# Last projections in three PSUM banks, frequency tables in another buffer, and halves exchanged by DMA in all fifteen regular frequency groups

## The chip, the cores and the metric

One NeuronCore of one Trainium2 chip runs the whole program. The metric is device time in microseconds (us) of one execution, from launch to end; lower is better. The kernel before took 462.2 us (median of 3 runs, 462.19 to 463.9). Its profiled execution took 462.63 us.

## The reference

The input is one sequence `x` of 2048 positions with 640 features, all in float32. Two branches are computed from it and mixed by a gate of each position.

```python
x = A_x
g = _sigmoid((x * gate_w).sum(-1, keepdims=True))
a = _A_ref(x, A_wqkv, A_wo)
b = _B_ref(x, B_w_r, B_w_i)
return g * a + (1 - g) * b
```

Branch A is attention with 32 heads of 20 features. Each position looks at 8 positions: itself and those 2, 4, ... 14 before it. `qkv = x @ wqkv`, softmax over the 8 logits, weighted sum of the values, and a last product with `wo` (640 x 640).

Branch B is a filter in the frequency domain: `irfft2(rfft2(x) * (w_r + 1j * w_i))` over positions and features, with one complex weight for each of 2048 x 321 frequencies.

## The kernel before, in words

**Tiling.** Position `16 p + j` lies on partition `p` (128 of them) in tile `j` (16 of them). Even and odd `j` are two halves of the attention (`par` 0 and 1), since a position looks only at positions of its own parity.

**Projections** (`qkv`, line 707). `wqkv` is cut into 4 column blocks `hg`. For each parity and block there are 8 tiles (`jj`), one PSUM bank each, with 15 matmuls of 128x128 by 128x480: the input and the weights are each split into a high and a low float32r part, and three of the four products are summed over 5 chunks of the features. Block 0 has two columns more, for the gate. A finished tile is copied by ScalarE (`ev`), together with its gate column (`z<-qkv`), and two tiles go to DRAM (`qkvd`) in one DMA of ScalarE's queue. There are two `ev` buffers, so a copy may wait for the DMA of the copy two before. Unit `u = 4 * par + hg`; the last unit to be recorded is u = 4 (odd tiles, block 0), whose tiles are named `qkv4_0` to `qkv4_7`. All units take their PSUM banks from one ring of seven, `BP`.

**Attention** (`attend`, line 745). For each parity and 8 head pairs, VectorE multiplies keys and queries and reduces them to logits `L`, GpSimd multiplies values by the softmax (`pv`), VectorE reduces these to `o`, and SP stores `o` to DRAM (`od`). It fills VectorE and GpSimd for most of the run.

**Filter.** `cols` (line 849) transforms each `x` tile over the partitions into `zg`, whose 128 columns of a tile are 16 groups of 8. `freq(g)` (line 871) carries one group through the rest; groups run in the order 1, 2, 3, 0, 4, ... 15, staged four deep. It gathers the group (`zc`), transforms the features (`v` and `u`, three matmuls each, in banks 0 and 1), adds and subtracts them (`ab`), and transforms over the 16 tiles with a table `tb` (`x` in bank 2, `z` in banks 3 and 4). A complex weight needs the real and the imaginary half of each result, which stand on partitions 0 to 63 and 64 to 127, and also the same result with the halves exchanged and one negated. There are two ways to get it. A group in `EXCHANGED` (1 to 8 before) multiplies `x` and `z` by a sign on ScalarE into `X` and sends `X` with two DMAs of ScalarE's queue to the other half of `P`. Every other group multiplies again on TensorE with the exchanged table (`ix` and `iz`). Then GpSimd multiplies `P` by the weights `wp` (three rows of 321 in an exchanged group, two in another) and adds, VectorE makes `z` and the sum and difference `s`, TensorE transforms back (`g`, bank 5), and ScalarE writes the group back into `zg`. A group that isn't exchanged has one VectorE multiply more (`t`).

The tables of three groups come in one load `mm` (960 columns). Before, `mm` shares the two buffers `ev0` and `ev1` with the projections' copies.

**Ends.** Even projections by `wo` (`project_even`, line 1079) need only attention of even tiles and are spread among the groups. When all groups are done, `spatial` (line 997) transforms `zg` back (`oa`, `ob`, `ha`, `hb`), first for odd, then for even tiles. Last come the odd projections (`project_odd`, line 1095): five transposes `oTp`, thirty matmuls `woa` and `wob`, two VectorE operations and a store for each of 8 tiles.

**What sets the order.** The program is not issued as it is written. Every operation is recorded with the data that it touches (`Plan.record`, line 223; in the profile every one of them has line 639, so rows are told apart by the names of their tiles). `Plan.order` (line 277) then draws 60 random changes of priority from a generator seeded with `SEED`, lays out each by a model with a duration for each kind of operation, and keeps the one that ends earliest. Each engine then runs its list in that fixed order, so an instruction that waits holds all behind it on its engine.

Of the kernel before, what the change touches and what calls it, by code (L numbers as in the profile page):

```python
# [24 lines left out]
PERM = np.array([0, 320] + list(range(2, 320, 2)) + list(range(1, 320, 2)))  # L25

BP = (0, 1, 2, 3, 4, 5, 6)
BV, BU, BX, BZ, BG, BO = (0,), (1,), (2,), (3, 4), (5,), (6,)
PAGE = 512

# [437 lines left out]
                exec(*op.call)  # L468


TURNS, AGAIN, MOVE, SEED = 6, 60, 2.0, 0
DRAWS, SOONEST, LATER_BY = 3, 2.4, 0.6
ENGS = ("PE", "DVE", "ACT", "POOL", "SP")
RATE = 380e3
# [29 lines left out]
class Mixer:  # L504
# [17 lines left out]
    def places(self, pp, dr, sb):  # L522
        self.pp, self.sb = pp, sb
        qb = self.pp.tile([128, 512], F32, tag="qbank", name="qbank")
        self.qthird = [qb[:, GC * i : GC * i + GC] for i in range(3)]
        self.qturn = -1
        self.qkv_d = dr.tile([8, 6, ROWS, HC], F32, tag="dram_qkv", name="qkvd")
        self.o_d = [dr.tile([128, 8, D], F32, tag=f"dram_o{i}", name=f"od{i}") for i in range(2)]
        self.f_d = dr.tile([128, 8, 2, D], F32, tag="dram_f", name="fd")
        self.a_d = dr.tile([128, 8, D], F32, tag="dram_a", name="ad")  # L530
        self.ident, self.fc = (self.one(n, 128) for n in ("ident", "fc"))
        self.fct = self.one("fct", 2, 128)
        self.z, self.g, self.ng, self.nng = (self.one(n, NJ) for n in ("z", "g", "ng", "nng"))
        make_identity(self.nc, self.ident)
        self.low = self.one("low", 64)
        self.nc.gpsimd.memset(self.low, -1e9)

        def ring(*tags):
            return Ring(sb, *tags)

        def n(tag, k):
            return ring(*(f"{tag}{i}" for i in range(k)))


        self.kvr, self.Lr, self.qr, self.prr = n("kv", 6), n("L", 3), n("q", 2), n("pr", 2)
        self.mr, self.sr, self.orr, self.pvr = n("m", 2), n("s", 2), n("o", 2), n("pv", 2)

        self.xr, self.wr, self.evr, self.rawr, self.fr = n("x", 8), ring(*WPLACES), n("ev", 2), n("raw", 5), n("f", 2)
        self.er = ring("e0", "e1")

        self.zcr, self.vsr, self.mdr, self.mfr, self.wpr = n("raw", 2), ring("raw2"), n("ev", 2), ring("mf"), n("f", 2)
        self.abr, self.Pr, self.s12r, self.Xr = ring("x0", "x1"), ring("x2", "x3"), ring("x4", "x5"), ring("raw3", "raw4")
        self.p1r = ring("x6")

        self.wor, self.war, self.yar = ring("ya", "w7"), n("w", 7), ring("ya")
        self.otr, self.oTr = (ring("w7"), ring("w7", "kv2")), (ring("x7"), ring("x7", "pr0"))
        self.osr, self.hor, self.hyr, self.yer = n("raw", 3), n("x", 4), ring("x4", "x5"), ring("x6")
        self.yr, self.yir = ring("raw3", "raw4", "e0", "ya"), n("f", 2)
        self.banks = {}
# [75 lines left out]
    def warm(self):  # L635
# [3 lines left out]
        p.dve.memset(w, 0.0)  # L639
        b = self.ps(BP, "warmed")  # L640
        for _ in range(6):
# [15 lines left out]
    def load_w(self, st, hg):  # L657
# [4 lines left out]
        for t in range(5):  # L662
# [8 lines left out]
            if hg == 1 and (t > 2 or 1 in self.xT) or (hg, t, 1 in self.xT) in W_DVE:  # L671
                b = self.ps(BP, f"ws{t}")[:, 0:n]
                p.act.copy(b, raw)
# [8 lines left out]
    def load_x(self, st, pair, j):  # L682
# [15 lines left out]
        if st is None and j in XO_DVE:  # L698
            for c in (0, 320):
                b = self.ps(BP, f"xs{j}_{c}")[:, 0:320]  # L700
                p.act.copy(b, raw[:, c : c + 320])
# [5 lines left out]
    def qkv(self, par, hg):  # L707
        p, d = self.p, self.qkv_d
        n = 482 if hg == 0 else 480
        u = 4 * par + hg  # L710
        for jj in range(8):
            j = 2 * jj + par
            hi, lo = self.xT[j]
            b = self.ps(BP, f"qkv{u}_{jj}")
            terms = []
            for t in (0, 2, 1, 4, 3) if u + jj == 0 else range(5):
                x = slice(128 * t, 128 * t + 128)
                if u == 0 and (jj, t) in WHOLE:
                    terms.append((self.xraw[j][:, x], self.wraw[hg, t]))
                else:  # L720
                    terms += [(a[:, x], w[hg][t]) for a, w in ((hi, self.wh), (hi, self.wl), (lo, self.wh))]
            for i, (a, w) in enumerate(terms):
                p.pe.matmul(b[:, 0:n], a, w, start=(i == 0), stop=(i == len(terms) - 1))
            if jj % 2 == 0:
                ev = self.evr.next(f"ev{u}_{jj}", 6, 2, HC)
            p.act.copy(ev[:, :, jj % 2], b[:, 0:480].rearrange("p (i c) -> p i c", i=6))
            if hg == 0:
                p.act.copy(self.z[:, j : j + 1], b[:, 480:481])
            if jj % 2:
                to = bass.AP(  # L730
                    tensor=d.tensor,
                    offset=d.offset + (6 * u * ROWS + 7 + jj - 1) * HC,
                    ap=[[8 * HC, 128], [ROWS * HC, 6], [1, 2 * HC]],
                )
                p.act.dma_start(to, ev.rearrange("p i j c -> p i (j c)"))
# [113 lines left out]
    def cols(self, q):  # L849
        p = self.p  # L850
        f = self.folded[q]
        for t0, n in ((0, 2), (2, 2), (4, 1)):
            z = self.ps(BP, f"z{q}_{t0}")
            for i in range(2 * n):
# [16 lines left out]
    def freq(self, g):  # L871
# [53 lines left out]
        A.copy(P[:, 0], x)  # L925
        if g in EXCHANGED:
            X = self.Xr.next(f"X{g}", 2, 321)
# [8 lines left out]
        yield  # L936
        n = 3 if g in EXCHANGED else 2
        G.tensor_mul(P[:, 0:n], P[:, 0:n], wp[:, 0:n])
        G.tensor_add(P[:, 0], P[:, 0], P[:, 1])
        if g in EXCHANGED:  # L940
            V.tensor_mul(z, z, wp[:, 3])
# [201 lines left out]

ON_ACT = ("vt", "q")

EXCHANGED = tuple(range(1, 9))

POOL_PR = {u: (6,) for u in ((0, 3), (0, 4), (0, 5), (0, 7), (1, 0), (1, 1), (1, 3), (1, 4), (1, 5), (1, 7))}

# [52 lines left out]
```

## Time and profile before

| | before |
|---|---|
| median of 3 runs | 462.2 us |
| the profiled execution | 462.63 us |
| its span, first to last instruction | 460.9 us |
| TensorE weight loads (PEld), busy | 393.6 us |
| ScalarE, busy | 210.0 us |
| DMA moved | 108.53 MB, mean 235 GB/s |

The profile names the engines PE (TensorE, with PEld for its weight loads), DVE (VectorE), ACT (ScalarE), POOL (GpSimd) and SP. A row `iz<-ab,mm` is an instruction that writes tile `iz` from `ab` and `mm`. A float32 matmul appears as two records, so a count of x2 is one matmul. "idle before" is the time in which the engine stood still ahead of an instruction, with what released it. ACTq and SPq are DMA issues.

### The profile page before, as it was taken

How to read it: one execution, taken by the hardware profiler on the slowest of the kernel's cores; microseconds unless marked ns; L12 is line 12 of the kernel's file. 1: busy time of each engine (PE TensorE's matmuls, PEld its weight loads, DVE VectorE, ACT ScalarE, POOL GpSimd, SP SyncE). 2: the span in 40 equal slices, each digit the busy share in tenths (PEclk: the TensorE clock that was granted, in tenths of full speed). 3: DMA queues.
4: the chain of work that ended last, by engine and by line, in shares of the span. 5: the costliest groups of instructions: out<-in, count | busy, mean ns of one | idle time of the engine just before them, and what ended most of it. 6: DMA issues, size and time to landing. Idle time of an engine off the chain costs nothing.

```text
span 460.9 us, 7237 instructions
## 1 busy us (share of the span) xinstructions
PE 448.6 (97%) x2465; PEld 393.6 (85%) x2465; DVE 416.4 (90%) x547; ACT 210.0 (46%) x547; POOL 324.3 (70%) x264
## 2 busy tenths in 40 slices
PE   7899999999999999999999989999999999999997
PEld 4688888888889889899887779988888999998996
DVE  4599959999999999999999999999999996989584
ACT  5432435453326454257348656656445554332120
POOL 1001644999999969999799899788787888952200
PEclk9999999999999999999999999999999999999999
DMA  8999998869697988869979998886362321546733
GB/s 297 409 367 319 390 373 269 272 190 304 174 281 227 321 260 281 263 199 295 327 216 256 295 283 240 246 280 215 115 207 74 114 70 58 165 111 197 233 110 114
DMA packets 73124, 108.53 MB, mean 235 GB/s; under 512 B 21104, under 2 KB 50800, under 8 KB 73088
## 3 DMA queue, kind: packets, MB, share of 16 engines
q1 hardware_dynamic: 40768, 69.90, 47.6%
q10 hardware_dynamic: 31408, 34.18, 23.7%
q0 software_dynamic: 912, 4.00, 2.2%
q8 instruction: 19, 0.31, 0.3%
q14 instruction: 17, 0.14, 0.1%
HBM read 72.59 MB, written 32.84 MB: 229 GB/s over the span
## 4 chain that ended last, share of the span: by engine, by line
PE 88%; DMA 4%; DVE 3%; POOL 2%; ACT 1%; issue 1%; SPq 0%; ACTq 0%; POOLq 0%; DVEq 0%
PE qkv L639 43%; PE wob L639 8%; PE woa L639 8%; PE z L639 6%; PE g L639 4%; PE ob L639 3%; PE oa L639 3%; PE v L639 3%; PE u L639 3%; PE x L639 2%; PE oTp L639 2%; DMA raw<-in_wqkv 2%; PE ha L639 2%; PE hb L639 1%; DMA st<-in_xT 1%; POOL P L639 1%
## 5 line engine op out<-in xcount | busy, mean ns | idle before, releaser
L639 PE MATMUL qkv<-w,xo 128*128 128x480 f32 (+1 forms) x480 | 107.8, 383 | 0.0
L639 PE MATMUL qkv<-w,xe 128*128 128x480 f32 (+1 forms) x465 | 102.9, 382 | 1.7 <-ACT xe L639 1.0
L639 PEld LDWEIGHTS qkv<-w,xe 128*128 128x128 f32 x465 | 87.3, 188 | 17.5 <-ACT xe L639 2.4
L639 PEld LDWEIGHTS qkv<-w,xo 128*128 128x128 f32 x480 | 89.9, 189 | 13.9
L639 ACT COPY ev<-qkv 128x480 f32<-128x480 f32 x64 | 35.5, 557 | 49.9 <-PE qkv L639 38.1
L639 PE MATMUL woa<-wo,oT 128*128 128x320 f32 x240 | 52.0, 318 | 0.0
L639 PE MATMUL wob<-wo,oT 128*128 128x320 f32 x240 | 51.5, 316 | 0.0
L639 PEld LDWEIGHTS woa<-wo,oT 128*128 128x128 f32 x240 | 39.4, 188 | 0.3
L639 PEld LDWEIGHTS wob<-wo,oT 128*128 128x128 f32 x240 | 39.2, 188 | 0.4
L639 POOL TENSOR_TENSOR P<-P,wp 128x963 f32<-128x963 f32 (+1 forms) x16 | 30.5, 1904 | 8.5 <-ACT P L639 3.7
L639 POOL TENSOR_TENSOR w<-raw,w 128x480 fp32r<-128x480 f32 (+1 forms) x20 | 25.2, 1278 | 12.6 <-ACT w L639 12.5
L639 POOL DMA_DIRECT2D fd<-fx x6 | 4.3, 717 | 39.8 <-DVE fx L639 39.8
L639 POOL TENSOR_TENSOR yi<-yi,y 128x640 f32<-128x640 f32 x8 | 12.5, 1557 | 22.1 <-DMA yi<-ad 12.9
L639 ACT CAST oT<-oTp 128x384 fp32r<-128x384 f32 (+1 forms) x32 | 13.4, 428 | 31.2 <-PE oTp L639 18.3
L639 PEld LDWEIGHTS g<-mm,s 128*128 128x128 f32 x150 | 21.4, 190 | 3.7 <-ACT zg L639 0.5
L639 PE MATMUL v<-bt,zc 128*128 128x321 f32 (+2 forms) x96 | 22.2, 347 | 1.9 <-ACT vs L639 1.0
L639 PE MATMUL oa<-gt,zg 128*128 128x161 f32 (+1 forms) x96 | 23.0, 344 | 0.0
L639 PE MATMUL g<-mm,s 128*128 128x128 f32 x150 | 22.9, 275 | 0.1
L639 PE MATMUL ob<-gt,zg 128*128 128x161 f32 (+1 forms) x96 | 22.5, 344 | 0.0
L639 PE MATMUL u<-bt,zc 128*128 128x321 f32 (+2 forms) x96 | 21.6, 344 | 0.0
L639 PEld LDWEIGHTS v<-bt,zc 128*128 128x128 f32 x96 | 16.1, 189 | 6.0 <-ACT vs L639 1.2
L639 ACT CAST w<-raw 128x480 fp32r<-128x480 f32 (+1 forms) x30 | 17.3, 592 | 8.1 <-PE qkv L639 3.3
(306 smaller groups left out, 1101.9 us busy)
## 6 DMA issues: line engine op xcount, KB each, us to landing
qkvd<-ev ACTq DMA_DIRECT2D x32, 480.0 KB, 5.7
wp<-in_ws SPq DMA_DIRECT2D x16, 642.0 KB, 4.9
raw<-in_wqkv SPq DMA_DIRECT2D x25, 240.0 KB, 7.1
fx<-in_x SPq DMA_DIRECT2D x8, 641.0 KB, 8.9
ot<-od SPq DMA_DIRECT2D x16, 320.0 KB, 3.2
fd<-fx POOLq DMA_DIRECT2D x6, 640.0 KB, 7.7
f<-fd SPq DMA_DIRECT2D x6, 640.0 KB, 6.1
P<-X ACTq DMA_DIRECT2D x16, 160.5 KB, 4.2
```

The costliest lines, as they stand in the source:

```text
L639: p.dve.memset(w, 0.0)
```

## The change

The diff is whole but for headers.

```diff
 BP = (0, 1, 2, 3, 4, 5, 6)
+BL = (4, 5, 6)
 BV, BU, BX, BZ, BG, BO = (0,), (1,), (2,), (3, 4), (5,), (6,)
...
-TURNS, AGAIN, MOVE, SEED = 6, 60, 2.0, 0
+TURNS, AGAIN, MOVE, SEED = 6, 60, 2.0, 2
...
-        self.zcr, self.vsr, self.mdr, self.mfr, self.wpr = n("raw", 2), ring("raw2"), n("ev", 2), ring("mf"), n("f", 2)
+        self.zcr, self.vsr, self.mdr, self.mfr, self.wpr = n("raw", 2), ring("raw2"), ring("x6", "ev0"), ring("mf"), n("f", 2)
         self.abr, self.Pr, self.s12r, self.Xr = ring("x0", "x1"), ring("x2", "x3"), ring("x4", "x5"), ring("raw3", "raw4")
-        self.p1r = ring("x6")
...
-            b = self.ps(BP, f"qkv{u}_{jj}")
+            b = self.ps(BL if u == 4 else BP, f"qkv{u}_{jj}")
...
-EXCHANGED = tuple(range(1, 9))
+EXCHANGED = tuple(range(1, 16))
```

The eight tiles of the last projection unit rotate through banks 4, 5 and 6 instead of seven, so that banks 0 to 3 are no longer held by them. The first table `mm1` goes to `x6` and the next to `ev0`, in turn. Groups 9 to 15 exchange halves by DMA: `ix` and `iz` are built for group 0 alone. The new seed draws other priorities for the whole program, so the lists of all engines differ from their start on. The program has 1985 matmuls before and 1971 after.

Three places of the new order follow. First, TensorE at the end of the last projection unit. `qkv4_7` is its last tile; `v`, `u`, `x` and `z` with a number are steps of that frequency group. Before:

```order
L639 MATMUL qkv4_7_323<-w0_2_293,xo15_196 128x482 x3
L639 MATMUL v2_612<-bt_325,zc2_611 128x321
L639 MATMUL x1_607<-ab1_605,mm1_599 128x321
L639 MATMUL z1_608<-ab1_605,mm1_599 128x321
L639 MATMUL v2_612<-bt_325,zc2_611 128x161
L639 MATMUL v2_612<-bt_325,zc2_611 128x160
L639 MATMUL u2_614<-bt_325,zc2_611 128x321
L639 MATMUL u2_614<-bt_325,zc2_611 128x161
L639 MATMUL u2_614<-bt_325,zc2_611 128x160
L639 MATMUL qkv4_7_323<-w0_3_295,xo15_196 128x482 x3
L639 MATMUL qkv4_7_323<-w0_4_297,xo15_196 128x482 x3
L639 MATMUL v3_623<-bt_325,zc3_622 128x321
```

After:

```order
L639 MATMUL v3_623<-bt_325,zc3_622 128x321
L639 MATMUL x2_618<-ab2_615,mm1_599 128x321
L639 MATMUL v3_623<-bt_325,zc3_622 128x161
L639 MATMUL v3_623<-bt_325,zc3_622 128x160
L639 MATMUL z2_619<-ab2_615,mm1_599 128x321
L639 MATMUL qkv4_5_320<-w0_4_297,xo11_192 128x482
L639 MATMUL u3_625<-bt_325,zc3_622 128x321
L639 MATMUL u3_625<-bt_325,zc3_622 128x161
L639 MATMUL u3_625<-bt_325,zc3_622 128x160
L639 MATMUL qkv4_7_323<-w0_1_291,xo15_196 128x482 x3
L639 MATMUL qkv4_7_323<-w0_2_293,xo15_196 128x482 x3
L639 MATMUL qkv4_7_323<-w0_3_295,xo15_196 128x482 x2
```

Before, group 3 starts after the last projection; now groups 1, 2 and 3 have their `v` and `u` behind them while 12 matmuls of `qkv4_7` are still to come.

Second, TensorE at the last groups. `woa` and `wob` are matmuls of an even projection, `oTp` its transposes, `g` a group's transform back. Before:

```order
L639 MATMUL g13_0_813<-mm13_776,s13_802 128x128 x3
L639 MATMUL oTp0_859<-ident_69,ot8_857 128x128 x3
L639 MATMUL iz14_815<-ab14_797,mm13_776 128x321
L639 MATMUL g13_3_814<-mm13_776,s13_802 128x128 x2
L639 MATMUL x15_819<-ab15_812,mm13_776 128x321
L639 MATMUL z15_820<-ab15_812,mm13_776 128x321
L639 MATMUL oTp3_860<-ident_69,ot8_857 128x128 x2
L639 MATMUL ix15_821<-ab15_812,mm13_776 128x321
L639 MATMUL g14_0_822<-mm13_776,s14_817 128x128 x3
```

After:

```order
L639 MATMUL g12_3_791<-mm10_730,s12_779 128x128 x2
L639 MATMUL oTp0_852<-ident_69,ot10_850 128x128 x3
L639 MATMUL z15_808<-ab15_802,mm13_770 128x321
L639 MATMUL g13_0_803<-mm13_770,s13_792 128x128 x3
L639 MATMUL oTp3_853<-ident_69,ot10_850 128x128 x2
L639 MATMUL g13_3_804<-mm13_770,s13_792 128x128 x2
L639 MATMUL g14_0_810<-mm13_770,s14_805 128x128 x3
L639 MATMUL woa10_855<-wo0_327,oT10_851 128x320 x3
```

`ix` and `iz` are gone. After these rows stand the rest of `woa10`, two of `g14`, all 15 of `wob10` and three transposes ahead of the first matmul of `g15`; between `z14` and `g14` stand 30 projection matmuls, five of `g12`, five of `g13`, `x15`, `z15`, a third of `u15` and five transposes.

Third, VectorE ahead of the odd projections. `h`, `ha` and `y` are the even tiles' spatial step, `o4b6` the last of the attention, `oT` the transposed rows for an odd projection. Before:

```order
L639 SCALAR_TENSOR_TENSOR ha12_980<-ha12_980,ng_74,h12_982 128x161
L639 TENSOR_TENSOR y12_987<-ha12_980,h12_982 128x321
L639 TENSOR_TENSOR oT1_996<-oTp3_998,oT1_996 128x256
L639 TENSOR_TENSOR y12_987<-ha12_980,h12_982 128x319
L639 SCALAR_TENSOR_TENSOR h14_990<-ha14_988,ng_74,h14_990 128x161
L639 SCALAR_TENSOR_TENSOR h14_990<-ha14_988,nng_75,h14_990 128x160
L639 TENSOR_TENSOR oT1_996<-oTp0_997,oT1_996 128x384
L639 TENSOR_TENSOR oT3_1002<-oTp3_1004,oT3_1002 128x256
```

After:

```order
L639 TENSOR_REDUCE o4b6_597<-pv4b6_598 128x160
L639 TENSOR_TENSOR oT1_982<-oTp3_984,oT1_982 128x256
L639 SCALAR_TENSOR_TENSOR h12_968<-ha12_966,ng_74,h12_968 128x161
L639 SCALAR_TENSOR_TENSOR h12_968<-ha12_966,nng_75,h12_968 128x160
L639 SCALAR_TENSOR_TENSOR h14_976<-ha14_974,ng_74,h14_976 128x161
L639 SCALAR_TENSOR_TENSOR ha12_966<-ha12_966,ng_74,h12_968 128x160
L639 TENSOR_TENSOR oT1_982<-oTp0_983,oT1_982 128x384
L639 SCALAR_TENSOR_TENSOR h14_976<-ha14_974,nng_75,h14_976 128x160
L639 TENSOR_TENSOR oT3_988<-oTp3_990,oT3_988 128x256
```

The first `oT1` has moved ahead of all of `h12` and `h14`, and part of tile 12 (its last `ha12` and both `y12`) behind it.

## The prediction

> **What bounds the kernel now.** I read the page's busy shares first, then a table by stage, then the chain that ended last, then the waits of TensorE.
>
> ```profile
> PE 448.6 (97%) x2465; PEld 393.6 (85%) x2465; DVE 416.4 (90%) x547; ACT 210.0 (46%) x547; POOL 324.3 (70%) x264
> ```
>
> TensorE is busy for 448.6 of 460.9 us and VectorE for 416.4, so either can set the end. Which of them does depends on the stage. In the next view the columns are the stretch, its length, and the busy time of PE, PEld, DVE, ACT and POOL, then the granted clock (1.00, full speed, throughout), the share of the DMA engines and GB/s.
>
> ```profile
> 0.00:22.00 22.00, 17.49 (x64) 11.97 (x64) 9.81 (x16) 10.76 (x20) 1.99 (x9) 1.00 0.94 351
> 22.00:100.00 78.00, 78.00 (x357) 67.23 (x358) 71.25 (x85) 33.50 (x83) 39.19 (x34) 1.00 0.90 313
> 100.00:234.00 134.00, 134.00 (x693) 117.92 (x692) 132.62 (x117) 59.16 (x159) 124.76 (x99) 1.00 0.85 263
> 234.00:255.00 21.00, 19.22 (x98) 15.34 (x96) 20.83 (x27) 13.80 (x42) 19.89 (x18) 1.00 0.92 267
> 255.00:275.00 20.00, 18.50 (x101) 14.99 (x102) 18.65 (x32) 12.44 (x38) 17.41 (x14) 1.00 0.93 284
> 275.00:350.00 75.00, 74.93 (x463) 66.01 (x463) 72.68 (x115) 42.22 (x116) 61.58 (x52) 1.00 0.70 217
> 350.00:380.00 30.00, 30.00 (x191) 27.55 (x190) 29.90 (x30) 16.45 (x44) 26.41 (x21) 1.00 0.24 71
> 380.00:420.00 40.00, 38.99 (x247) 35.46 (x246) 33.06 (x66) 16.86 (x38) 28.36 (x22) 1.00 0.41 120
> 420.00:461.00 41.00, 37.51 (x263) 37.14 (x261) 27.63 (x68) 4.85 (x13) 4.70 (x3) 1.00 0.51 161
> ```
>
> From 22 to 234 us TensorE never stops. It stands 1.78 and 1.50 us in the two stretches in which the projections end and the groups begin, then runs without a break to 400. VectorE runs nearly as full until 380, then has slack. To see that a busy TensorE here is work and not waiting, I read pieces of the chain in the stage of the groups (start, length, what):
>
> ```profile
> 300.42 0.22 PE g L639 x2
> ...
> 303.81 0.54 PE iz L639 x2
> ...
> 305.12 0.22 PE oTp L639 x2
> ...
> 309.23 2.21 PE woa L639 x15
> ```
>
> The chain of that stage is TensorE throughout, matmul against matmul. So a matmul taken out of it is time off the span, as long as nothing else becomes late.
>
> **Matmuls removed.** Seven groups (9 to 15) lose `ix` and `iz`. The grouped rows of TensorE say how many that is, 14 records of each, two records a matmul:
>
> ```profile
> L639 PE MATMUL ix<-ab,mm 128*128 128x321 f32 x14 | 5.1, 444 | 0.0
> ...
> L639 PE MATMUL iz<-ab,mm 128*128 128x321 f32 x14 | 4.9, 434 | 0.0
> ```
>
> The 434 to 444 ns of a record overlap with the next record, so I price by the chain: 0.54 us a matmul. 14 x 0.54 = 7.6 us less, all of it from a stretch (275 to 350) in which TensorE is busy for 74.93 of 75 us.
>
> **Work put in their place.** The multiply of `P` on GpSimd grows from two rows of weights to three. ScalarE copies once less and signs twice, and VectorE loses `t`:
>
> ```profile
> L639 POOL TENSOR_TENSOR P<-P,wp 128x963 f32<-128x963 f32 x8 | 17.9, 2243 | 4.6 <-DMA P<-X 2.6 <-ACT L6a L639 1.5 <-ACT X L639 0.5
> ...
> L639 POOL TENSOR_TENSOR P<-P,wp 128x642 f32<-128x642 f32 x8 | 12.5, 1565 | 3.8 <-ACT P L639 3.7
> ...
> L639 ACT ACTIVATE X<-x,sign 128x321 f32<-128x321 f32 x8 | 4.3, 532 | 1.6 <-PE x L639 1.4
> ...
> L639 ACT COPY P<-ix 128x321 f32<-128x321 f32 x8 | 3.4, 427 | 3.8 <-PE ix L639 3.8
> ```
>
> The view of tile `t` gives minimum, median and maximum in ns, and the first and last start:
>
> ```profile
> L639 DVE TENSOR_TENSOR t<-z,wp x8: 481/484/490, 262.9 to 341.5; 128x321 f32<-128x321 f32 x8
> ```
>
> GpSimd gets 7 x (2.243 - 1.565) = 4.7 us more. In 275 to 350 it is busy for 61.58 of 75 us, which leaves 13.4 us; I cost it at nothing, and at up to 4.7 us if the attention's `pv`, queued behind it, has no slack. ScalarE gets 7 x (2 x 0.532 - 0.427) = 4.5 us and 14 DMA issues, beside 42.22 of 75 us busy: nothing. VectorE gets 7 x 0.484 = 3.4 us back.
>
> One rule of the Trainium skill speaks against the longer GpSimd multiply. SBUF — State Buffer, section "Who interferes with whom", says that a VectorE instruction with two SBUF inputs is shut out for the whole of a GpSimd instruction that reads SBUF. Read as if it held for every VectorE instruction, it would charge the 4.7 us to VectorE as well, and its 3.4 us gain would become a loss of 1.3; where VectorE sets the end, the time by it would be 462.2 + 1.3 = 463.5 us. By its own condition it spares the multiplies of the groups, whose other input is in PSUM, and the row of `t` agrees: 481 to 490 ns eight times over, beside a GpSimd that is busy 82% of that stretch.
>
> **The longer way of a half.** An exchanged half returns later than a matmul did, and TensorE's list is fixed, so the distance in its list between `z` and `g` must cover the way. The last exchanged group before, group 8, shows the whole way:
>
> ```profile
> 291.64 0.70 PE L639 MATMUL z<-ab,mm 128*128 128x321 f32 x2
> ...
> 292.39 0.53 ACT L639 ACTIVATE X<-z,sign 128x321 f32<-128x321 f32 x1
> ...
> 292.99 1.12 ACTq L639 DMA_DIRECT2D P<-X  x2
> ...
> 299.08 2.24 POOL L639 TENSOR_TENSOR P<-P,wp 128x963 f32<-128x963 f32 x1 [2.59 <-DMA P<-X]
> ...
> 302.18 0.89 DVE L639 TENSOR_TENSOR s<-P,z 128x321 f32<-128x321 f32 x2 [0.33 <-POOL P L639]
> ```
>
> For all 16 such DMAs the view of tile `X` has, from issue to landing:
>
> ```profile
> DMA to landing us min/median/max: 2.5/4.2/6.3
> ```
>
> `z` is through at 291.64 + 0.54 = 292.2 and `s` at 303.1: 10.9 us, with a second half that took about 5.5 us from its issue (293.5 to 299.0). At the median 4.2 the way is 9.6 us, at the minimum 2.5 it is 7.9. In the list after, the part on the change shows what stands before `g14` and `g15`. By the chain's prices that is, from `z14` to `g14`, 30 projection matmuls (4.4), ten `g` (2.2), `x15` and `z15` (1.1), five transposes (0.55) and a bit of `u15` (0.25): 8.5 us. From `z15` to `g15` it is 4.4 + 2.2 + 0.55 = 7.2 us. A wait at `g14` also helps `g15`, so the two waits together are the way less 7.2: 2.4 us at the median, 0.7 at the minimum, 3.7 as group 8 had it. I take 2.4. It has no cover: behind these groups stands `spatial`, which needs all of them. Groups 9 to 13 have over 11 us of other work in between and cost nothing.
>
> **Groups among the last projections.** TensorE's waits in 234 to 275 are three:
>
> ```profile
> PE g L639 <- DVE s L639: 1.4, 1, 1.4
> ...
> PE v L639 <- ACT vs L639: 1.0, 1, 1.0
> ...
> PE v L639 <- ACT zc L639: 0.9, 1, 0.9
> ```
>
> They are nearly all of the 1.78 + 1.50 = 3.3 us that TensorE stands there. The first is group 0, which had two short matmuls between `iz0` and `g0` and now has other groups' work of over 4 us: it goes. The others come from groups that start one after the other with nothing else to run; now projections lie between them (the first piece of the order), but `v4` and `v5` follow as before, so I count half of 1.9. Gain 2.3 us, between 0 and 3.3.
>
> **Three banks.** The fourth tile to use the ring, `qkv4_3`, shares bank 4 with `qkv4_0` and stands only two projection matmuls and two transforms (4 x 0.22 = 0.9 us) behind it, while ScalarE has to copy the tile and its gate column out (0.56 us for the tile in the row below, and whatever ScalarE is at when the tile ends): I take 0.5 us lost. The other reuses lie further apart. It can be worse, since ScalarE has stood still here:
>
> ```profile
> 216.11 17.84 PE L639 MATMUL qkv<-w,xo 128*128 128x482 f32 x80
> ...
> 227.00 0.56 ACT L639 COPY ev<-qkv 128x480 f32<-128x480 f32 x1 [5.08 <-DMA qkvd<-ev]
> ```
>
> and in the list of waits (in total, times, longest):
>
> ```profile
> ACT ev L639 <- DMA qkvd<-ev: 11.6, 4, 5.1
> ```
>
> ScalarE waited 5.08 us for an earlier store of `ev`, and TensorE ran through it on other banks. So the bound is 0 to 5.1 us.
>
> **The rest.** The first table now stands on SP's list between the loads `f6` and `f7`, and waits there for `qkv4_0`, the last reader of its buffer. The median loads, from issue to landing:
>
> ```profile
> f<-fd SPq DMA_DIRECT2D x6, 640.0 KB, 6.1
> ...
> mm<-in_t_mm SPq DMA_DIRECT2D x5, 480.0 KB, 3.7
> ```
>
> `f7`, held behind it, needs a buffer that `z5` gives free only a matmul later, and 30 projection matmuls (6.7 us) and ten transforms (2.2) follow before `z7` reads it: 8.9 us against 6.1, so nothing. The table itself is read some 20 us later. The new seed redraws all lists. TensorE has no idle time from 22 to 234 to win back, and 4.5 us of start (22 - 17.49) in which it waits for loads; I take nothing, with 1.5 us either way.
>
> Sum against the profiled execution's 462.63 us: -7.6 - 2.3 + 0.5 + 2.4 = -7.0, so 455.6; the median is 0.4 lower than that execution, so 455.2 us.
>
> **The rivals.** First, VectorE sets the end. It is behind TensorE where the odd projections start:
>
> ```profile
> 411.40 1.39 DVE o4b L639
> ...
> 417.86 0.58 DVE h L639 x2
> 418.44 0.47 DVE oT L639
> ...
> 418.96 0.55 PE oTp L639 x3
> ```
>
> VectorE's own longest wait in that stretch, from the list of waits:
>
> ```profile
> DVE h L639 <- ACT h L639: 1.6, 1, 1.6
> ```
>
> The chain runs through VectorE from 408 to 419, and a TensorE that comes 7 us sooner meets a VectorE that has gained 3.4. For it: VectorE is busy for 132.62 of 134 and 29.90 of 30 us. Against: the third piece of the order moves the last `ha12`, `y12` and half of `h14` behind the second `oT1` (0.4 + 0.9 + 0.3 = 1.6 us, at the 0.58 us of two `h` and like rows beside it), and the wait of 1.6 us on ScalarE follows from TensorE's own pace, so it should go when TensorE is early. Together with 3.4 that is 6.6 of the 7 us. If neither helps, only 3.4 us are won: 459.2 against the profiled execution, 458.8 against the median.
>
> Second, the three banks decide, on the other side. Unit 4 has four `ev` halves, and if ScalarE is held 5.1 us at each with three banks, a tile of 15 matmuls (17.84 / 80 x 15 = 3.3 us) covers 3.3 of it and 1.8 remain, plus 0.7 for the copies: 10.0 us in all, and then the groups' first steps come late by as much and the 2.3 us are lost too. -7.6 + 2.4 + 10.0 = +4.8: 467.0. It turns slower than no change from 5.2 us of such waits on. Against it: in the new list the store of an `ev` and the copy that waits for it lie 20 rows apart on ScalarE. The trace before cannot show three banks at work. The Trainium skill, Perfetto Trace Analysis, section "Matmuls", has independent groups of matmuls rotate through different PSUM banks, so that copying one out overlaps the next; by that rule, going from seven banks to three moves towards this rival, and the 17.84 us without a stop beside a 5.08 us wait of ScalarE agree with it.
>
> Third, the new draw puts holes into the stretch from 22 to 234, which has none: VectorE is at 132.62 of 134 there, and a shift of it or of GpSimd (124.76) by 3% leaves TensorE waiting 5 to 7 us. Then nothing is gained: 462.
>
> Fourth, the change doing nothing it says is ruled out for the matmuls, whose count falls by 14; the groups' early start could fail if `wp1` or `mm1` land late, which takes back 2.3 us: 457.5, inside the forecast.
>
> **How the numbers follow.** About 0.5% (2.3 us) is what a measurement of this kernel can tell from no change. The forecast has 0.66, VectorE at the end 0.16, holes from the draw 0.10, the banks 0.08. The forecast's own range is 451.0 (waits of the groups all gone, 0.7 for the halves, 1.5 won at the start: -7.6 - 3.3 + 0.7 - 1.5 = -11.7) to 459.0 (3.7 for the halves, no gap won). Up to 460.5 it takes in VectorE at the end and leaves out the two last, 0.18. Faster: 0.66 and most of the second, 0.79. Same: 0.13, from the second and third. Slower: 0.08.
>
> **What would show it.** Right: TensorE's busy time about 6 us less with `ix` and `iz` at 4 records each; its idle time in the stretch after the projections under 2 us; a wait of 1 to 4 us on `s` at `g14` or `g15`; VectorE's wait rows before `oT` no longer on the chain. Wrong: a TensorE idle share that rises between 22 and 234, waits of `qkv` on ScalarE's `ev`, or odd projections that wait for `o4b` or `oT` by more than 3 us.

## The result, and the profile after

The kernel after takes 461.76 us (median of 20 runs), the kernel before 463.88 us in the same sessions (20 runs; the three runs that stood ahead of the prediction had a median of 462.2). The ratio is 0.9945, 95% interval 0.9931 to 0.996: 2.55 us faster, where 7.0 us were forecast. Put on the 462.2 us of the prediction that is 459.7 us. The profiled execution after took 462.29 us with a span of 460.5, so the two traces differ by only 0.4 us of span and are read stage by stage.

The page's busy row, and the grouped rows of `ix` and `iz`:

```profile
PE 446.6 (97%) x2437; PEld 390.1 (85%) x2437; DVE 416.9 (91%) x540; ACT 212.5 (46%) x554; POOL 329.1 (71%) x264
```
```profile
L639 PE MATMUL ix<-ab,tbfirst 128*128 128x321 f32 x4 | 1.4, 433 | 0.0
...
L639 PE MATMUL iz<-ab,tbfirst 128*128 128x321 f32 x4 | 1.2, 434 | 0.0
```

The 28 records are gone, yet TensorE is busy for only 2.0 us less. That is how a busy time adds up, not work that stayed: the record of a matmul ends later than the next matmul can start (a `z` lasts 0.70 us, and the next starts after 0.54), so a gap in the work is partly covered by the record ahead of it. An estimate from the starts alone, the number of records of each shape times their median distance to the next start, puts TensorE's work at 440.0 us before and 432.5 after. That is 7.5 us less, as priced. So the matmuls went, and what has to be explained is the time that TensorE stands still in their place.

The table by stage (stretch, its length, busy time of PE, PEld, DVE, ACT, POOL):

```profile
100.00:234.00 134.00, 133.51 (x690) 117.28 (x690) 132.57 (x118) 59.75 (x159) 124.21 (x98) 1.00 0.87 265
...
234.00:255.00 21.00, 21.00 (x105) 17.50 (x104) 20.45 (x29) 13.94 (x43) 19.78 (x18) 1.00 0.82 227
255.00:275.00 20.00, 19.33 (x108) 15.37 (x106) 19.07 (x31) 14.04 (x43) 18.32 (x16) 1.00 0.95 325
275.00:350.00 75.00, 71.03 (x443) 62.37 (x443) 71.52 (x107) 42.95 (x120) 64.92 (x48) 1.00 0.84 255
350.00:380.00 30.00, 28.16 (x171) 24.70 (x172) 28.57 (x29) 16.48 (x45) 26.91 (x22) 1.00 0.24 71
```

Between 234 and 275 TensorE's idle time fell from 3.28 to 0.67 us, as forecast. But in 275 to 380, where it had stood for 0.07 us, it now stands for 3.97 + 1.84 = 5.8 us (counted from the starts, as above, 0.8 before and 9.6 after). From 22 to 234, where the third rival put its holes, it stands for only 0.49 us. What it waits for from 234 to 380 (in total, times, longest):

```profile
PE z L639 <- DVE s L639: 1.6, 2, 1.0
PE oTp L639 <- DVE oT L639: 1.5, 2, 1.0
PE g L639 <- DVE s L639: 1.0, 2, 0.8
PE oTp L639 <- ACT ya L639: 0.8, 2, 0.6
PE g L639 <- ACT zg L639: 0.7, 2, 0.5
PE oa L639 <- ACT zg L639: 0.6, 1, 0.6
```

VectorE, which was to win 3.4 us from the lost `t`, now waits in 275 to 380 for the products of the exchange, 3.3 us:

```profile
DVE z L639 <- POOL P L639: 2.6, 3, 1.6
...
DVE s L639 <- POOL P L639: 0.7, 2, 0.3
```

The chain that ended last shows both. First at group 6: its half lands after 7.10 us, and the `z` of group 8, which uses the same one of the two `z` banks, waits for the `s` that frees it (start, length, what):

```profile
280.11 7.10 DMA P<-X
287.43 2.24 POOL P L639
289.75 0.76 POOL P L639
290.53 0.90 DVE s L639 x2
291.47 0.81 PE z L639 x2
```

Then at group 15, where the chain leaves TensorE for more than ten microseconds:

```profile
339.36 0.77 PE z L639 x2
...
341.26 6.59 DMA P<-X
...
348.07 2.26 POOL P L639
...
351.18 0.50 DVE s L639
...
351.82 0.92 PE g L639 x6
```

The first `oa`, where the groups give way to `spatial`, starts at 353.29 us instead of 348.78. By then six even projections are done instead of five, and one costs 2 x 2.21 + 0.55 = 5.0 us by the rows of the prediction, while two `g` are still to come (0.44). In work done the two kernels are level there, where the kernel after should have been 7 us ahead.

Of the signs that the prediction named, `ix` and `iz` at 4 records each, the 0.67 us after the projections and a short wait of `g` for `s` came. TensorE's busy time fell by 2.0 us and not by about 6, and the chain still passes through VectorE ahead of the odd projections (from 409.83 to 418.5 us).

### The profile page after: what moved, and what is told of

It is laid out like the page before. It is cut to its first block, busy times and chain, and to the rows that moved or that the text cites. A ratio compares the mean times of both kernels' runs of the same rounds, so it can differ in the third digit from the quotient of the medians.

```text
span 460.5 us, 7204 instructions
## 1 busy us (share of the span) xinstructions
PE 446.6 (97%) x2437; PEld 390.1 (85%) x2437; DVE 416.9 (91%) x540; ACT 212.5 (46%) x554; POOL 329.1 (71%) x264
## 4 chain that ended last, share of the span: by engine, by line
PE 57%; DVE 6%; DMA 3%; issue 2%; POOL 1%; ACT 1%; ACTq 0%; DVEq 0%; POOLq 0%
PE qkv L639 17%; PE woa L639 7%; PE wob L639 7%; PE z L639 5%; PE ob L639 3%; PE oa L639 3%; DMA P<-X 3%; PE u L639 3%; PE v L639 3%; PE g L639 3%; PE hb L639 2%; PE oTp L639 2%; PE ha L639 1%; PE x L639 1%; POOL P L639 1%
## 5 line engine op out<-in xcount | busy, mean ns | idle before, releaser
L639 PE MATMUL qkv<-w,xo 128*128 128x480 f32 (+1 forms) x480 | 120.2, 392 | 0.0
L639 PE MATMUL qkv<-w,xe 128*128 128x480 f32 (+1 forms) x465 | 104.5, 381 | 0.0
L639 PEld LDWEIGHTS qkv<-w,xo 128*128 128x128 f32 x480 | 88.6, 189 | 12.7
L639 PE MATMUL wob<-wo,oT 128*128 128x320 f32 x240 | 46.5, 316 | 0.2 <-ACT ya L639 0.2
L639 PE MATMUL woa<-wo,oT 128*128 128x320 f32 x240 | 46.6, 318 | 0.0
L639 POOL TENSOR_TENSOR P<-P,wp 128x963 f32<-128x963 f32 (+1 forms) x16 | 35.3, 2205 | 8.3 <-ACT oT L639 3.0
L639 PEld LDWEIGHTS wob<-wo,oT 128*128 128x128 f32 x240 | 37.7, 188 | 0.9 <-ACT ya L639 0.4
L639 PEld LDWEIGHTS woa<-wo,oT 128*128 128x128 f32 x240 | 37.5, 188 | 0.5 <-ACT oT L639 0.2
L639 PE MATMUL oa<-gt,zg 128*128 128x161 f32 (+1 forms) x96 | 21.1, 345 | 0.6 <-ACT zg L639 0.6
L639 PEld LDWEIGHTS u<-bt,zc 128*128 128x128 f32 x96 | 16.2, 190 | 3.8 <-PE v L639 0.4
```

## The experiments

All ratios are against the kernel before, run alternately on the same chip, with 95% intervals; 0.001 is 0.46 us. Three theories were on trial. A: the long way of an exchanged half, with two `z` banks and two `P` buffers, takes the gain back. B: the new draw of the order lost it. C: VectorE is as full as TensorE in the stage of the groups, so a matmul less on TensorE is not time off the span. The runs no_turn, same_order_way, same_order_both, same_order_bare, order8_vector and bare_vector leave out work that the result needs: they are there to measure, not to be used.

| run | what | ratio |
|---|---|---|
| all15_old | before, 15 groups exchanged | 1.005 (1.0032 to 1.0069) |
| draw2_old | before, seed 2 | 1.0027 (1.0009 to 1.0045) |
| eight_new | after, groups 1 to 8 exchanged | 0.9978 (0.9961 to 0.9996) |
| draw0_new | after, seed 0 | 0.9986 (0.9969 to 1.0003) |
| no_turn | eight_new without 14 matmuls, redrawn | 0.9924 (0.9898 to 0.995) |
| three_three | after, three z banks and P buffers | 0.9998 (0.9972 to 1.0024) |
| light_fifteen | after, VectorE lighter, redrawn | 1.0049 (1.0026 to 1.0071) |
| light_eight | eight_new, VectorE lighter, redrawn | 0.9958 (0.9937 to 0.9978) |
| same_order_way | order of after, copies for DMAs | 0.9909 (0.989 to 0.9928) |
| same_order_light | order of after, VectorE lighter | 0.9905 (0.9884 to 0.9926) |
| same_order_both | both | 0.9893 (0.9872 to 0.9913) |
| same_order_bare | order of eight_new, 14 matmuls out | 0.996 (0.9939 to 0.9981) |
| order8_vector | order of eight_new, VectorE 10.8 us lighter | 0.9966 (0.9947 to 0.9985) |
| bare_vector | the last two together | 0.9904 (0.9872 to 0.9935) |
| same_order_nomax | order of after, no maximum | 0.9908 (0.9887 to 0.993) |

### The parts of the change, and the draw

```diff
# all15_old: the kernel before
-EXCHANGED = tuple(range(1, 9))
+EXCHANGED = tuple(range(1, 16))
# draw2_old: the kernel before
-TURNS, AGAIN, MOVE, SEED = 6, 60, 2.0, 0
+TURNS, AGAIN, MOVE, SEED = 6, 60, 2.0, 2
# eight_new: the kernel after
-EXCHANGED = tuple(range(1, 16))
+EXCHANGED = tuple(range(1, 9))
# draw0_new: the kernel after
-TURNS, AGAIN, MOVE, SEED = 6, 60, 2.0, 2
+TURNS, AGAIN, MOVE, SEED = 6, 60, 2.0, 0
```

> The kernel before with one line changed: all 15 regular groups exchange; seed 0, seven banks and the old buffers stay. Theory A (the z banks): an exchanged group holds one of the two z banks from its z matmul to its s, about 13 us, so two banks let a group pass every 6.8 us whatever TensorE saves; then this kernel lies between 0.993 and 1.003 of the kernel before, with z waiting for s on TensorE and 6.5 to 7 us from z to z in the groups after group 4. Theory B (the draw): the exchange is worth its 7 us, and the draw of seed 2 lost most of it; then this one, with seed 0, comes out near 0.985.

> The kernel before with seed 2 and nothing else. Theory A: the draw is worth little, 0.996 to 1.004 of the kernel before. Theory B: the draw of seed 2 costs the 4 to 5 us that the change failed to win, 1.009 to 1.011.

> The kernel after with groups 1 to 8 alone exchanged, as before; three banks, the new buffers and seed 2 stay. It shows what these are worth without the exchange in groups 9 to 15. Theory A: 0.993 to 1.002 of the kernel before, no wait of z for s in groups 10 to 15. Theory B: 1.000 to 1.011, as the draw of seed 2 would cost as much here.

> The kernel after with seed 0. Theory A: as the kernel after, 0.991 to 0.999 of the kernel before, again with 6.5 to 7 us from z to z. Theory B: 0.985.

The exchange alone, on the kernel before, is slower: 1.005, above what either theory had; the other three lie in the ranges of A. The pairs that differ in the three banks and the tables' new places (and, through them, in the order that the planner finds) favour these: 0.9978 against 1.0027 with seed 2 and eight groups, 0.9986 against 1.005 with seed 0 and fifteen, 2.3 and 3.0 us. The seed alone is worth +1.2 us on the kernel before and -1.9 us on the kernel after, with either sign, so B as it was put (the draw of seed 2 cost 4 to 5 us) falls. But a redraw moves the time by as much as what is looked for here. Comparisons across a redraw therefore carry an error of 2 us and more that no interval shows, and the 2.3 and 3.0 us are no larger than it.

### Taking the matmuls, the buffers or VectorE's work away, redrawn

```diff
# no_turn, on eight_new
-            A.copy(P[:, 1], col(BX, "ix", 0, 1))
+            A.copy(P[:, 1], x if g else col(BX, "ix", 0, 1))
-            iz = col(BZ, "iz", 1, 1)
+            iz = z if g else col(BZ, "iz", 1, 1)
# three_three, on the kernel after
-BV, BU, BX, BZ, BG, BO = (0,), (1,), (2,), (3, 4), (5,), (6,)
+BV, BU, BX, BZ, BG, BO = (0,), (0,), (2,), (1, 3, 4), (5,), (6,)
-        self.abr, self.Pr, self.s12r, self.Xr = ring("x0", "x1"), ring("x2", "x3"), ring("x4", "x5"), ring("raw3", "raw4")
+        self.abr, self.Pr, self.s12r, self.Xr = ring("x0", "x1"), ring("x2", "x3", "ev1"), ring("x4", "x5"), ring("raw3", "raw4")
# light_fifteen on the kernel after, light_eight on eight_new
+        self.m0 = self.one("m0", 8, 4)
+        self.nc.gpsimd.memset(self.m0, 0.0)
...
-        m = self.mr.next(f"m{nm}", 8, 4)
-        V.tensor_reduce(out=m, in_=L, axis=AX.X, op=ALU.max)
+        m = self.m0
```

> The kernel after with groups 1 to 8 exchanged, and groups 9 to 15 without the matmuls ix and iz and with nothing in their place: they multiply x and z themselves, so these seven groups compute something else. The 14 matmuls go, and no group takes a longer way. Theory A (the 13 us hold of two z banks and two P buffers eats the gain): the bare matmuls are worth their 7.6 us against the run eight_new (0.9978), 0.981 to 0.985 of the kernel before. Theory C (TensorE's time is not what sets the end, VectorE and the chains between the engines are): 0.993 to 0.998.

> The kernel after with three banks for z (v and u share one) and three buffers for P, the third in ev1. Theory A: z and P no longer make a group wait, TensorE gets most of its 5.8 us of idle time between 275 and 380 back, 0.983 to 0.988. Theory C: the waits for s go but others come in their place, 0.992 to 0.999.

> The kernel after without the maximum of the softmax on VectorE (a tile of zeros is subtracted in its place): 16 reductions of 0.41 us, 6.6 us of VectorE. Read against light_eight. Theory C in the form that VectorE is next: the exchange pays once VectorE is lighter, this one 4 us or more under light_eight. Theory A: it stays 0 to 3 us under it, as the pair with the full VectorE (0.9945 and 0.9978).

> The kernel after with groups 1 to 8 alone exchanged, and without the maximum of the softmax on VectorE, as in light_fifteen. Theory C in the form that VectorE is next: 0.990 to 0.997 of the kernel before. Theory A: the same, since the lighter VectorE lets this one win as much as light_fifteen.

Leaving the 14 matmuls out, with no exchange in their place, won 2.5 us against eight_new, not 7.6: a little more than C had, and far from A, by which the bare matmuls are worth their price.

In three_three, where `z` has a third bank because `v` and `u` share one, the wait of `z` for `s` is gone from TensorE's list, but `g` waits for the same `s` instead (in total, times, longest):

```profile
PE g L639 <- DVE s L639: 5.0, 5, 2.7
```

The ratio is 0.9998, no gain; but the shared bank and the new order are in it too, so it does not settle what a third bank alone is worth. The pair with a lighter VectorE fits neither theory: 0.9958 and 1.0049 lie further apart, and the other way round, than either said, each with a new draw. How much a draw can do shows in light_fifteen: it has no more to do than same_order_light below, which keeps the order of the kernel after, and takes 6.7 us longer (1.0049 and 0.9905). After this pair the order was held fixed.

### The same order, one thing changed

The planner lays out the unchanged program, and the call of an operation is replaced only when it is issued. The edits are shortened; group 0 keeps its matmuls, and in same_order_bare a group still takes the bank of the `iz` that it doesn't write.

```diff
+    def instead(self, fn, *a):
+        code, _ = self.ops[-1].call
+        self.ops[-1].call = (code, {"fn": fn, "a": a, "k": {}})
# same_order_way
             A.dma_start(P[0:64, 1:3], X[64:128])
+            p.instead(self.nc.scalar.copy, P[0:64, 1:3], X[0:64])
             A.dma_start(P[64:128, 1:3], X[0:64])
+            p.instead(self.nc.scalar.copy, P[64:128, 1:3], X[64:128])
# same_order_light
         V.tensor_reduce(out=m, in_=L, axis=AX.X, op=ALU.max)
+        p.instead(self.nc.vector.memset, m, 0.0)
# same_order_both: both of these
# same_order_bare, on eight_new: its order is kept as a list, groups 9 to 15 lose two matmuls each
-            A.copy(P[:, 1], col(BX, "ix", 0, 1))
+            A.copy(P[:, 1], x)
-            V.tensor_mul(z, z, wp[:, 2])
+            V.tensor_scalar_mul(z, t, 2.0)
```

> The kernel after with every list in the same order, but in the place of the two DMAs of an exchange two ScalarE copies of half the partitions each, so the halves are not exchanged and the result differs; the way from z to s loses its 5 to 8 us between X and P. It takes the draw out of the question. Theory A (the way is the whole loss): TensorE's waits in the stage of the groups go and the end comes 4 to 6 us earlier, 0.981 to 0.986 of the kernel before. Theory C (VectorE stands right behind, so whatever TensorE saves is lost again ahead of the odd projections): 1.5 to 3 us, 0.988 to 0.991, with VectorE without a stop from 400 to 419.

> The kernel after in the same order, but the 16 maxima of the softmax on VectorE are replaced by a short memset, so VectorE has about 5 us less to do. Theory A: no gain while the way holds TensorE, 0.993 to 0.996. Theory C: a gain of 1 to 3 us, 0.988 to 0.992.

> Both edits of same_order_way and same_order_light, again in the order of the kernel after. Theory A: as same_order_way, 0.981 to 0.986. Theory C: clearly more than either alone, 0.978 to 0.984, since the two hold each other.

> The kernel of eight_new in exactly its order, with the 14 matmuls ix and iz of groups 9 to 15 left out and nothing in their place (P takes x, and a multiply of t by a constant stands in for the one of iz, so these groups compute something else). It prices the term of 7.6 us by itself. If a matmul taken out of TensorE's list is time off the span: 7.6 us under eight_new, 0.981 to 0.983 of the kernel before. If VectorE takes over in the tail: 2 to 4 us under it, 0.989 to 0.994.

With copies for the DMAs, 1.7 us are won on the kernel after; with VectorE lighter, 1.9; with both, 2.4. A had 4 to 6 us for the first and none for the second. C has the sizes of both single runs, but not of the pair, which it put at 5 us or more. Its sign, VectorE without a stop from 400 to 419, didn't come either: there VectorE is busy for 16.71 of 19 us in same_order_way.

The run same_order_way is a weaker test than it looks. Its copies keep ScalarE busy for 22 us more (234.6 against 212.5), and the way hardly got shorter: from `z` to the end of `s`, groups 4 to 15, it takes 12.2 us on average instead of 12.8. At group 15 the copies are done at 340.43 us, and GpSimd's multiply still starts only at 344.76, because an instruction of the attention stands ahead of it on GpSimd and waits for VectorE's `o6b`:

```profile
343.47 1.48 POOL L643 TENSOR_TENSOR pv5a<-vt5a,L5a 128x640 f32<-128x640 f32 x1 [2.37 <-DVE o6b L643]
344.76 2.28 POOL L643 TENSOR_TENSOR P<-P,wp 128x963 f32<-128x963 f32 x1
```

So there, with the DMAs gone, the order of GpSimd's list and VectorE's pace hold `P` in their place.

The plainest answer is same_order_bare: 14 matmuls out of TensorE's list and nothing else in its order changed, 0.996 against 0.9978, 0.8 us (the profiled spans differ by 1.4). The two intervals overlap, so this is little or nothing. The stretch 275 to 350 of eight_new:

```profile
275.00:350.00 75.00, 74.66 (x455) 65.03 (x454) 72.39 (x116) 41.26 (x114) 63.04 (x52) 1.00 0.71 221
```

And of same_order_bare, where TensorE stands 4.74 us, most of it for VectorE's `ab` (counted from the starts, its idle time grows from 2.0 to 8.9 us, nearly by what the matmuls gave):

```profile
275.00:350.00 75.00, 70.26 (x428) 60.22 (x428) 72.77 (x117) 41.37 (x115) 62.54 (x52) 1.00 0.69 220
```
```profile
PE x L653 <- DVE ab L653: 3.0, 3, 1.2
```

The chain that ended last there, which ran through TensorE alone in the kernel before and through VectorE from 299 to 317 us in eight_new, is VectorE's for most of the way from 282 to 338, instruction behind instruction, attention and filter mixed:

```profile
302.45 1.39 DVE L5a L653
303.85 1.39 DVE o6a L653
...
306.97 1.39 DVE o6a L653
308.36 1.39 DVE pr5b L653
309.75 0.40 DVE ab L653
310.16 0.40 DVE iz L653
...
312.75 1.39 DVE L5b L653
```

### Is it VectorE's load in that stage?

```diff
# order8_vector on eight_new, bare_vector on same_order_bare; both in the order of eight_new
+            if nm in ("5a", "5b"):
+                p.instead(self.nc.vector.memset, L[:, jj : jj + 2].rearrange("p j h r -> p j r h"), 0.0)
```

> The kernel of eight_new in exactly its order, with the eight reductions to logits of heads 5a and 5b (1.48 us each, from 283 to 333) replaced by short memsets, so those heads' logits are zero: VectorE has 10.8 us less to do in the stage of the groups, TensorE as much as before. If TensorE and VectorE hold the stage together: little alone, 0 to 2 us under eight_new, 0.994 to 0.998 of the kernel before. If VectorE alone holds it: 5 us or more under it, 0.987 or less.

> The same eight reductions replaced in the kernel of same_order_bare (the 14 matmuls out, same order). If VectorE's load is what took the matmuls' 7.6 us back: 5 us or more under same_order_bare at the end of the groups, and 3 to 6 us at the end, 0.983 to 0.989. If the cause is elsewhere: 0 to 2 us, 0.991 to 0.996.

VectorE's time out of the stage alone: 0.9966, 0.6 us under eight_new. The matmuls alone: 0.8. Both: 0.9904, 3.4 us. That lies between the two ranges that were expected, and the intervals by themselves would still allow the plain sum of 1.4; the traces are clearer. They must be read from a common point, since the four already differ by up to 1.7 us at the `z` of group 4, before any edit takes effect. That `z` and the first `oa`, in eight_new, same_order_bare, order8_vector and bare_vector:

```profile
264.90 0.71 PE L639 MATMUL z<-ab,mm 128*128 128x321 f32 x2
349.06 1.25 PE L639 MATMUL oa<-gt,zg 128*128 128x322 f32 x6
```
```profile
264.26 0.70 PE L653 MATMUL z<-ab,mm 128*128 128x321 f32 x2
347.77 1.25 PE L653 MATMUL oa<-gt,zg 128*128 128x322 f32 x6
```
```profile
263.23 0.70 PE L643 MATMUL z<-ab,mm 128*128 128x321 f32 x2
347.18 1.25 PE L643 MATMUL oa<-gt,zg 128*128 128x322 f32 x6
```
```profile
264.63 0.71 PE L657 MATMUL z<-ab,mm 128*128 128x321 f32 x2
344.12 1.25 PE L657 MATMUL oa<-gt,zg 128*128 128x322 f32 x6
```

From the one to the other it takes 84.16 us in eight_new, 83.51 without the matmuls, 83.95 with the lighter VectorE and 79.49 with both: 0.65, 0.2 and 4.7 us less. The first two are within what the four differ by anyway (up to 1.3 us from the first `z` of the groups to that of group 4); the third is not, and it is far more than the sum of the two. With VectorE's load out of the way the same 14 matmuls are worth 4.5 us (83.95 - 79.49). From the first `oa` to the end the four take 112.8 to 113.0 us: what the stage of the groups wins arrives at the end, and nothing is lost ahead of the odd projections.

In the stretch 275 to 350 of order8_vector, then of bare_vector:

```profile
275.00:350.00 75.00, 74.60 (x455) 64.99 (x454) 62.96 (x116) 41.06 (x115) 63.29 (x53) 1.00 0.67 220
```
```profile
275.00:350.00 75.00, 73.03 (x453) 63.61 (x452) 66.65 (x120) 42.73 (x121) 66.68 (x55) 1.00 0.71 224
```

With VectorE lighter, TensorE has no slack to use (74.60 of 75). With TensorE lighter, VectorE has little (72.77). With both, TensorE's wait for `ab` is gone from the list, and its idle time falls from 4.74 to 1.97 us. So VectorE's load in that stage is what holds back most of the matmuls' gain, though not all: against same_order_bare the groups end 3.7 us earlier (4.0 from the common point), where 5 or more were expected, and 7.6 us of matmuls and 10.8 us of VectorE's work together bring 3.4 us by the ratio and 4.8 by the profiled spans (461.9 and 457.1).

### A faster version

```diff
# same_order_nomax, on the kernel after, in its order: neither is issued
-        V.tensor_reduce(out=m, in_=L, axis=AX.X, op=ALU.max)
-        G.tensor_sub(L, L, m.unsqueeze(3).broadcast_to([128, 8, 4, 8]))
```

> The kernel after in its order, without the maximum of the softmax and without its subtraction on GpSimd: the softmax is the same up to rounding, since these logits are small. VectorE has 6.6 us less, GpSimd 16 times 0.63 = 10 us less. If VectorE and GpSimd hold TensorE back: under same_order_light (0.9905), 0.984 to 0.989. If not: as same_order_light, 0.989 to 0.992.

0.9908: it beats both kernels, as same_order_light does (0.9905); their intervals lie just below that of the kernel after. But the 10 us of GpSimd that it saves bring nothing more. The run didn't show GpSimd holding TensorE back. Leaving out the maximum is safe only where the logits stay small.

## Why the prediction was wrong, point by point

**The step that failed** is the first: "So a matmul taken out of it is time off the span, as long as nothing else becomes late." The chain of waits went through TensorE, and that was read as if TensorE alone set the pace. The same table had VectorE at 72.68 of 75 us in that stage: 2.3 us of slack against a gain of 7.6. A chain names one way through the work; it doesn't say how close the next one is. The price of the matmuls was right (7.5 us of work gone, by the starts); that this is time off the span was not. Taken out alone, they shortened the run by 0.8 us in an unchanged order (same_order_bare; 0.65 in its stage) and 2.5 in a new one (no_turn). What took the gain back there, in the traces, is VectorE: with 10.8 us less of its work the same matmuls are worth 4.5 (bare_vector). That the measured 459.7 us lies under the 460.5 up to which the prediction counted a gain is no merit of its sum. (The ends of the forecast's range, 451.0 and 459.0, are 450.5 and 458.8 by its own terms on the median; nothing hangs on that.)

**The first rival** (VectorE sets the end, 458.8 us, chance 0.16) came nearest: 459.7 by the ratio. It was right about the engine and wrong about the place, so its number is near by luck. It was placed only ahead of the odd projections. The chain does run through VectorE there, in the kernel after too, but nothing is lost there: from the first `oa` to the end it takes 106.9 to 107.4 us in the kernel after and the four runs in its order, though that `oa` starts up to 3.9 us earlier in them. VectorE holds TensorE already in the stage of the groups, from 282 us on in the chain of same_order_bare, and there the prediction gave it no price.

**VectorE's 3.4 us** from `t` were won in its list (the row of `t` now has one instruction) and lost in waits of 3.3 us for `P`: a half that lands late stops VectorE, and behind it the attention. Over the whole run VectorE's busy time did not fall at all (416.4 and 416.9 us): rows outside this stage grew, one `fe` alone from 0.82 us to 3.48 beside two GpSimd instructions at 49 us.

**The longer way** was put at 9.6 us from the median landing of 4.2 us. The view of tile `X` after:

```profile
DMA to landing us min/median/max: 2.5/4.7/7.1
```

At group 15 it is 351.82 - 339.95 = 11.9 us from the end of `z` to `g` and 12.1 to the end of `s`, 2.5 more than forecast and more than group 8 had (10.9). TensorE's waits between the two, `oTp` for `oT` and `ya`, `wob` for `ya`, `g` for `zg` and `s`, are 1.03 + 0.20 + 0.46 + 0.17 + 0.62 + 0.82 = 3.3 us, against 2.4 forecast and an upper bound of 3.7. That fits only as a sum: the wait for `s` itself, which the term priced, is 0.82 us, and the rest are waits for other work, which the term did not have. What was missing too is that an exchanged group keeps its `z` in the bank, updated in place, until `s` has read it (group 13: from 326.25 to 339.25, 13.0 us), while a group with `iz` lets it go after `t` and then needs the other bank, for `iz`, only a short time (group 9 before: from 303.65 to 307.08). Two banks then let a group pass in half that time, 6.5 us and the slip between. From `z4` to `z15`:

```profile
264.13 0.81 PE L639 MATMUL z<-ab,mm 128*128 128x321 f32 x2
...
339.30 0.81 PE L639 MATMUL z<-ab,mm 128*128 128x321 f32 x2
```

(339.30 - 264.13) / 11 = 6.8 us a group, and the `z` of groups 8, 11 and 15 start 0.06 us after the end of the `s` that frees their bank. With two banks and that hold the exchange can hardly be faster. But it is also the pace of the kernel before (6.9, from 263.56 to 339.39) and of same_order_bare (6.8), where the groups without an exchange hold a bank for less. So more banks alone need not make the groups faster; no run tests them alone.

Perfetto Trace Analysis of the Trainium skill, section "Identifying the Most-Contended Engine", has the engine with the highest occupancy optimized first, and for TensorE it does not trust the matmuls' busy share but looks, beside the arithmetic done, at that of the weight loads. By the weight loads TensorE stands at 85% before and VectorE at 90%, so the rule points at VectorE, where the prediction went by TensorE's 97%. The runs agree in part: TensorE made lighter alone gave 0.8 us, but VectorE made lighter alone (order8_vector) gave no more, 0.6; it took both.

**The groups among the last projections** were right: 2.3 us forecast, and 3.28 - 0.67 = 2.6 us less idle time in 234 to 275.

**Three banks** cost nothing that shows in the kernel after: no `qkv` waits for an `ev`, and the rival that they decide didn't come. That depends on the order, though: in eight_new ScalarE is held 4.46 us by the store of an `ev`, and a `qkv` then waits 1.2 us for the copy of a gate column. That is the mechanism of the rival, at a small price. The pairs of old and new banks and tables differ by 2.3 and 3.0 us, where the prediction had 1.8 for these two terms together; each pair is also a redraw.

**The draw** was put at nothing, with 1.5 us either way. It is +1.2 and -1.9 us in the two pairs that differ in the seed alone, and 6.7 us between light_fifteen and same_order_light.

**What stays open**: why same_order_both, with neither the DMAs nor VectorE's maxima, still ends only 2.4 us earlier (the wait of GpSimd for `o6b`, above, was seen at one group and not taken away); how the 9.6 us that TensorE stands in the kernel after divide among the exchange, VectorE and the new order, since the runs that show VectorE's part have no exchange in groups 9 to 15; and how much of the 2.55 us belongs to the exchange in this draw. After against eight_new says 1.5 us, all15_old says that it costs 2.3, and light_fifteen against light_eight 4.2; the draw lies in all three.

## What to carry to other kernels

Before a term "so many instructions at so much each" is taken off the span, compare it with the slack of the second engine in the same stretch, not with the chain alone: where two engines are over 95% busy and feed each other, as here, expect no more than the other engine's slack until both get less work. Where a planner draws the order anew, hold the order and replace single calls; it separates a few microseconds of cause from as many of luck. Compare such traces from a common point ahead of the first edit. A tile that is updated in place keeps its bank for the whole round trip, so divide the round trip by the number of banks before lengthening it.

## What the runs showed of the hardware

The same VectorE instruction on 128x16 numbers, `ng`, took 0.40 us before and 1.11 us after. Before, with GpSimd beside it:

```profile
272.81 2.24 POOL L639 TENSOR_TENSOR P<-P,wp 128x963 f32<-128x963 f32 x1
```
```profile
274.68 0.40 DVE L639 TENSOR_SCALAR ng<-g 128x16 f32<-128x16 f32 x1
```

And after:

```profile
306.63 1.42 POOL L639 TENSOR_TENSOR pv6a<-vt6a,L6a 128x640 f32<-128x640 f32 x1
```
```profile
306.98 1.11 DVE L639 TENSOR_SCALAR ng<-g 128x16 f32<-128x16 f32 x1
```

Each ends within 0.05 us of the GpSimd instruction that was already running (275.08 beside 275.05, 308.09 beside 308.05), whatever its own size. SBUF — State Buffer of the Trainium skill, section "Who interferes with whom", has a `tensor_scalar` able to take the port pair shared with GpSimd, and lets the one that comes second block in full; these rows agree. The `tensor_tensor` rows with one input in PSUM are not stretched: `s` has a median of 0.48 us before and after.
